# An S4 convolution block in float32 on one core: the prologue's step tables and sines in another order, the rows' first transform stage on 64 by 64 tiles, and the last block's inverse over all channels

## The chip, the cores and the metric

The kernel runs on one core of one Trainium2 chip. The metric is the device time of one execution in microseconds, as the median of several runs; the profile is one more execution with the hardware profiler on. PE is the matrix engine (PEld its weight loads), ACT, DVE and POOL are the scalar, vector and GpSimd engines, and SP issues most transfers. Each engine works through its own instruction list in order; engines wait for each other by semaphores.

## The reference, cut to what matters

A layer norm with a modulation from `silu(c) @ w_mod`, a long convolution per channel with a kernel `K` that is built from 192 complex modes, a residual, and then a second modulated layer norm with a bilinear GLU. L is 2048, D is 640, F is 1536.

```python
mod = (_silu(c) @ w_mod).reshape(c.shape[0], 6, 1, -1)
sa, ca, ga, sb, cb, gb = (mod[:, 0], ...)
h = _layernorm(x, axis=-1) * (1 + ca) + sa
# _A_ref(h): per channel d
dt = jnp.exp(log_dt)[:, None]
P = jnp.exp((dt * A)[:, :, None] * l[None, None, :])
K = jnp.einsum("dn,dnl,dn->dl", Cc, P, dt * Bc).real
y = irfft(rfft(h padded to 2L) * rfft(K padded to 2L))[:L] + h * Dskip
x = x + ga * y
h = _layernorm(x, axis=-1) * (1 + cb) + sb
x = x + gb * (((h @ w_gate) * (h @ w_up)) @ w_down)
```

## The kernel before

The 640 channels are five blocks (`db`) of 128. The 2L-point transform is done as two matrix stages, 32 by 64.

*Kernel generation.* For 40 groups `n` of 16 channels the values of `K` come from outer products of two short tables per channel: POOL multiplies out the phases (`mk_ph`, tile `Ph`) and the amplitudes (`mk_eq`, `mk_ep`, tiles `EQ` and `EP`, two buffers each, taken in turn), ACT takes sines and cosines of the phases (`trig`, PSUM tiles `tra` and `trb`), DVE multiplies amplitude and sine (tiles `QtA`, `PtA`, `QtB`, `PtB`), and PE contracts over the modes (`kg_ma`, `kg_mb`, tile `kg`). The short tables come from `u_seeds(db)`, once for each block: steps named by letters, in the order of the strings `SEG0` (block 0) and `SEG` (the others). `a` to `d` make the phase step, `r` and `R` the decay steps of the block's two halves, `e` and `E` their exponentials (`LP`, `RH`, `RL`), `x` to `f` the amplitude and the angle of a mode, `g` and `h` transpose them, and `v` turns them into the start values. `tab_ph` and `tab_eq` then double the steps into tables on POOL; `weighted` (lines 637 and 638) waits for `v` there.

*Rows.* `u_stats` loads a slab of x and takes its statistics on DVE, `u_hm` normalises it on ACT and stores it to `hm` in DRAM. `u_pre(db, q)` loads a quarter of a block from `hm` and runs the first stage of the row transform on PE: 32 by 32 tiles, for a real and an imaginary part, and the same again with one contraction row for the shift (`t_one`). The result goes to `FH` in DRAM. `u_g(db, qd)` reads a quarter of the frequencies back, runs the second stage (`stage2`, line 876) and keeps the spectra in place in the tile `gh` (three buffers).

*Product and way back.* `u_k(n)` is the first stage for `K`, into the tile `f16` (two buffers). `u_c(db, qd)` runs the second stage for `K`, multiplies with the row spectra on DVE (six operations, lines 911 to 922), runs the first inverse stage on PE (line 930), and writes to `WD` in DRAM. `u_d(db, c)` reads `WD` across, runs the last inverse stage (line 951), adds x and writes `x2d`. In the last block `u_c` is called twice for each quarter, for 64 channels each: eight units, each with its own second stage, product, inverse and write.

*GLU.* `u_head` loads the first four row slabs of `x2d` as `xb`, takes the remaining statistics when `u_d(4, 0)` has come, and starts the up projections (`psg`, lines 973 to 975). Then 48 rounds (line 1281) of up and down projections follow, each in three products of split operands.

*What sets the order.* The loop over `t` (line 1153) runs through the generation, three steps for each `n`. Everything else is cut at its `yield`s, and the table `SCHED` gives each piece a due time: `due(x)` (line 1084) issues all pieces whose time lies in bucket x, two buckets of ten for each step `t`. Times below zero lie in the prologue, one bucket for each step of `u_seeds(0)`; times from 2400 on lie behind the last generation step. `SLOT` gives the buffer letter of each allocation. So the table fixes, for each engine and for the transfer queues of SP and ACT, what is issued behind what.

## Time and profile before

| | us |
|---|---|
| median of the three runs | 1056.52 |
| the runs | 1050.58, 1058.03, 1056.52 |
| the profiled execution, its own time | 1050.8 |
| its span in the trace | 1049.0 |
| PE busy | 941.2 (90%) |
| DVE busy | 645.8 (62%) |
| ACT busy | 575.5 (55%) |
| POOL busy | 410.2 (39%) |

The shares of the whole span say little, because the kernel has four stages in a row: the prologue until the first sines (about 34 us), the generation with the transforms of the first four blocks beside it (to about 465 us), the rest of the last block and the head of the GLU (to 547 us), and the GLU rounds. In the last stage PE works without a gap, POOL works only up to the end of the generation.

The page's slices, 40 of 26 us each, show the four stages at a glance: for POOL the busy digits end where the generation ends, and the clock row shows where PE was granted less than full speed.

```profile
PE   4834899898789798998689999999999999999998
DVE  8678468797978997874555544535445263444242
ACT  4849989887888889852233244332443234433231
POOL 4976789699779989920026000000000000000000
PEclk9878699799889899998779999999999999999999
```

### The profile page before, as it was taken

The page shows a single profiled execution, that of the slowest core. Times are in us where ns is not written, and L with a number is a line of the kernel's source. Part 1 is how long each engine was busy: PE and PEld are TensorE (multiplying, and loading weights), DVE is VectorE, ACT ScalarE, POOL GpSimd, SP SyncE. Part 2 cuts the span into 40 slices and gives each one's busy share as a digit, 9 for nine tenths or more (in the row PEclk, how much of TensorE's full clock was granted, in tenths as well). Part 3 has the DMA queues.
Part 4 walks back from the last instruction along what each step waited for, and adds up shares of the span by engine and source line. Part 5 has one row for each costly group of instructions (what it writes and reads, how often), then busy time and mean ns, then how long its engine had stood idle before and what let it go on. Part 6 is the DMA issues. An engine that isn't in the chain of part 4 may idle for free.

```text
span 1049.0 us, 27184 instructions
## 1 busy us (share of the span) xinstructions
PE 941.2 (90%) x11750; PEld 771.4 (74%) x11750; DVE 645.8 (62%) x1216; ACT 575.5 (55%) x1027; POOL 410.2 (39%) x268
## 2 busy tenths in 40 slices
PE   4834899898789798998689999999999999999998
PEld 2623666676576577777548888888888888888887
DVE  8678468797978997874555544535445263444242
ACT  4849989887888889852233244332443234433231
POOL 4976789699779989920026000000000000000000
PEclk9878699799889899998779999999999999999999
DMA  7537657255435553577569000100002000010001
GB/s 252 215 88 249 209 186 223 68 156 157 130 115 163 163 169 109 168 224 216 148 197 367 24 1 1 62 39 1 1 1 101 1 1 1 1 51 1 1 1 51
DMA packets 118456, 113.00 MB, mean 108 GB/s; under 512 B 16192, under 2 KB 99904, under 8 KB 117696
## 3 DMA queue, kind: packets, MB, share of 16 engines
q1 hardware_dynamic: 108864, 108.25, 32.4%
q10 hardware_dynamic: 9472, 3.02, 1.1%
q8 instruction: 92, 1.51, 0.6%
q14 instruction: 28, 0.23, 0.1%
HBM read 74.48 MB, written 36.77 MB: 106 GB/s over the span
## 4 chain that ended last, share of the span: by engine, by line
PE 68%; ACT 15%; DVE 10%; issue 4%; DMA 3%; SPq 1%; DVEq 0%; ACTq 0%
PE acc L1256 16%; PE psg L973 11%; PE psg L975 10%; PE psg L974 10%; PE psfc L876 2%; PE psfb L876 2%; ACT trb L227 2%; ACT tra L227 2%; PE psfb L930 2%; ACT L227 2%; PE psfa L876 2%; PE psfc L930 1%; PE kg L809 1%; PE kg L794 1%; ACT LP L227 1%
## 5 line engine op out<-in xcount | busy, mean ns | idle before, releaser
L1233 DVE TENSOR_TENSOR pr<-psg,gsb 128x512 f32<-128x512 f32 x48 | 33.2, 691 | 203.5 <-issue 147.5
L697 POOL TENSOR_TENSOR EQ<-LQ,RH 128x1536 f32<-128x1536 f32 x40 | 124.3, 3106 | 20.6 <-DVE QtB L754 20.2
L227 ACT ACTIVATE ah<-pr 128x512 fp32r<-128x512 f32 x48 | 30.4, 632 | 150.9 <-DVE pr L1233 150.9
L973 PE MATMUL psg<-hh,wsgh 128*128 128x512 f32 x240 | 96.1, 401 | 1.0 <-ACT hh L227 1.0
L974 PE MATMUL psg<-hh,wsgl 128*128 128x512 f32 x240 | 94.1, 392 | 0.0
L975 PE MATMUL psg<-hl,wsgh 128*128 128x512 f32 x240 | 94.1, 392 | 0.0
L974 PE MATMUL psg<-hh,wsul 128*128 128x512 f32 x240 | 94.0, 392 | 0.0
L973 PE MATMUL psg<-hh,wsuh 128*128 128x512 f32 x240 | 93.9, 391 | 0.0
L975 PE MATMUL psg<-hl,wsuh 128*128 128x512 f32 x240 | 93.7, 391 | 0.0
L1256 PE MATMUL acc<-wsdl,ah 128*128 128x384 f32 (+1 forms) x384 | 88.2, 309 | 0.0
L1256 PE MATMUL acc<-wsdh,al 128*128 128x384 f32 (+1 forms) x384 | 88.1, 309 | 0.0
L1256 PE MATMUL acc<-wsdh,ah 128*128 128x384 f32 (+1 forms) x384 | 87.9, 308 | 0.0
L227 ACT ACTIVATE gsb<-psg 128x512 f32<-128x512 f32 x48 | 28.4, 592 | 99.3 <-PE psg L975 99.3
L697 POOL TENSOR_TENSOR EP<-LP,RH 128x768 f32<-128x768 f32 x40 | 66.1, 1653 | 0.0
L697 POOL TENSOR_TENSOR Pha<-LH,DH 128x1536 int32<-128x1536 int32 (+1 forms) x21 | 62.5, 2974 | 6.6 <-ACT trb L227 6.2
L1256 PEld LDWEIGHTS acc<-wsdh,ah 128*128 128x128 f32 x384 | 62.2, 188 | 3.8
L697 POOL TENSOR_TENSOR Phb<-LH,DH 128x1536 int32<-128x1536 int32 x20 | 62.3, 3115 | 1.8 <-ACT tra L227 1.8
L1256 PEld LDWEIGHTS acc<-wsdl,ah 128*128 128x128 f32 x384 | 58.9, 188 | 0.0
L1256 PEld LDWEIGHTS acc<-wsdh,al 128*128 128x128 f32 x384 | 58.8, 188 | 0.0
L968 DVE TENSOR_TENSOR al<-pr,ah 128x512 fp32r<-128x512 f32 x48 | 34.4, 717 | 33.5 <-ACT ah L227 33.5
L975 PEld LDWEIGHTS psg<-hl,wsgh 128*128 128x128 f32 x240 | 45.1, 188 | 10.9 <-DVE hl L1015 1.1
L809 PEld LDWEIGHTS kg<-QtB,PtB 64*32 64x32 f32 x2560 | 41.4, 113 | 15.6 <-issue 7.5
(516 smaller groups left out, 2523.8 us busy)
## 6 DMA issues: line engine op xcount, KB each, us to landing
TVa<-WD SPq DMA_DIRECT2D x28, 256.0 KB, 3.4
t_tw<-w_mod SPq DMA_DIRECT2D x3, 1600.0 KB, 7.9
t_ti<-w_mod SPq DMA_DIRECT2D x3, 1600.0 KB, 7.8
ghb<-FH SPq DMA_DIRECT2D x8, 512.0 KB, 4.7
WD<-Wb SPq DMA_DIRECT2D x8, 512.0 KB, 3.4
WD<-Wa SPq DMA_DIRECT2D x8, 512.0 KB, 4.0
wg<-B_w_gate SPq DMA_DIRECT2D x6, 640.0 KB, 9.5
wu<-B_w_up SPq DMA_DIRECT2D x6, 640.0 KB, 10.7
```

What stands on the lines that cost most here:

```text
L227: return S.activation(o, i, f, **kw)
L697: G.tensor_tensor(o.rearrange("p x (h l) -> p x h l", l=8), lo.unsqueeze(2).to_broadcast([P, rows, nh, 8]), hi.rearrange("p h x -> p x h") ...
L794: PE.matmul(kg[j * 32 : j * 32 + 32, dd, :], PtA[:, c, dl * 4 + j, :], QtA[:, c, dl * 4 + j, :], start=dd == 0 and c == 0, stop=False, til ...
L809: PE.matmul(kg[j * 32 : j * 32 + 32, dd, :], PtB[lo : lo + 64, c, r, :], QtB[lo : lo + 64, c, r, :], start=False, stop=dd == 7 and c == 1, ...
L876: PE.matmul(r[c][par * 64 : par * 64 + 64, i, :], t_tw[:, k0 + k, c, :], src[:, k, :], start=True, stop=True, tile_position=(0, par * 64))
L930: PE.matmul(r[par][:, i, :dn], t_ti[lo : lo + 64, qd * 4 + i, c, :], x[lo : lo + 64, i, :], start=n == 0, stop=n == len(pro) - 1, tile_pos ...
L968: V.tensor_tensor(lo, v, hi, op=OP.subtract)
L973: PE.matmul(ps, wh, xh, start=start, stop=False)
L974: PE.matmul(ps, wl, xh, start=False, stop=False)
L975: PE.matmul(ps, wh, xl, start=False, stop=stop)
L1233: V.tensor_tensor(pr, r[1], gsb, op=OP.mult)
L1256: PE.matmul(o[c], x[:, ts], w[:, cs], start=st, stop=ft == NF - 1 and n == 2 and (c == 0 or t % 2 == 1))
```

## The change

The change has four parts and a new table of due times.

1. *Prologue.* The step `E` (exponentials of block 0's second half) leaves the prologue and becomes a piece of its own (`LATE`, due at 150, in the generation's step 7). The amplitude is computed first in `s_f`; a new step `G` transposes it before the arctangent, and ACT instead of DVE copies it into `RL`. `tab_ph` computes the third phase step for only the half that it works on, so block 0 has one more short POOL operation. The identity matrix comes by a transfer of its own instead of an ACT copy, and the constants come in three transfers instead of one.
2. *Rows.* `u_pre` runs its first stage in 64 by 64 tiles with weights that hold two slabs each, eight products instead of sixteen for each quarter and block.
3. *Last block.* `u_c` is one unit for each quarter with two second stages and two products of 64 channels, written in place into the row spectra, and then one inverse, one evacuation and one write over all 128 channels. The row spectra of the last block lie in one `f16` buffer (`GL`) instead of four `gh` buffers.
4. *Order.* All due times and buffer letters are new. Of the table the diff below shows the due times of the seeds of blocks 2 and 3, one number for each step of `SEG`.

```diff
-SEG0 = ("l", "a", "b", "c", "ud", "r", "x", "e", "f", "g", "D", "h", "v", "R", "E")
+SEG0 = ("l", "a", "b", "c", "ud", "r", "x", "e", "f", "G", "g", "D", "h", "v", "R", "")
...
-    tab=(475, 761),
+    tab=(526, 788),
...
+    e0=(150,),
...
-        (375, 435, 587, 674, 684, 684, 716, 751, 825, 825, 844, 868, 874, 882),
-        (880, 973, 1167, 1241, 1254, 1260, 1312, 1324, 1350, 1355, 1358, 1358, 1360, 1369),
...
+        (375, 582, 589, 670, 671, 677, 723, 786, 824, 825, 826, 845, 861, 863),
+        (984, 1169, 1224, 1242, 1264, 1267, 1286, 1292, 1336, 1336, 1343, 1343, 1345, 1349),
...
+            V.scalar_tensor_tensor(amp, u, dt2[:, db : db + 1], pe[:, 1], op0=OP.mult, op1=OP.mult)
             V.scalar_tensor_tensor(pe[:, 0], pe[:, 0], 1e-37, u, op0=OP.max, op1=OP.add)
             V.reciprocal(pe[:, 0], pe[:, 0])
-            V.scalar_tensor_tensor(amp, u, dt2[:, db : db + 1], pe[:, 1], op0=OP.mult, op1=OP.mult)
...
-        def s_g():
+        def s_G():
...
             trans(amp, T["ps2"][:, 0])
+            if db == 0:
+                for h in range(2):
+                    act(g4(Rl[h])[:, 3], T["ps2"][:, 0, hs[h]])
+
+        def s_g():
+            if db:
+                s_G()
             act(y, y, AF.Arctan)
...
+        if db == 0:
+            LATE.append(lambda: s_e(1))
...
-        if a != 0:
-            G.tensor_tensor(dh[:, 3], dh[:, 1], dh[:, 2], op=OP.add)
+        G.tensor_tensor(sel(dh[:, 3]), sel(dh[:, 1]), sel(dh[:, 2]), op=OP.add)
...
-            for j in range(4):
-                a = slice(32 * j, 32 * j + 32 if i == 0 else 32 * j + 1)
+            for j in range(2):
+                a = slice(64 * j, 64 * j + 64 if i == 0 else 64 * j + 1)
                 for c in range(2):
-                    o = 32 * (j ^ (2 * c))
-                    PE.matmul(r[c][o : o + 32], (t_s1h, t_one)[i][a, c], h[a] if i == 0 else shr[a, d0].unsqueeze(1).to_broadcast([1, 4, P]),
-                              start=i == 0, stop=i == 1, tile_position=(32 * j, o))
+                    o = 64 * (j ^ c)
+                    PE.matmul(r[c][o : o + 64], (t_s1h, t_one)[i][a, c], h[a] if i == 0 else shr[a, d0].unsqueeze(1).to_broadcast([1, 4, P]),
+                              start=i == 0, stop=i == 1, tile_position=(64 * j, o))
...
-        Gt = ring(fp, [P, 8, P], "gh")
+        if db < NB - 1:
+            Gt = ring(fp, [P, 8, P], "gh")
+        else:
+            if db not in GL:
+                GL[db] = ring(f16, [P, 32, P], "f16")
+            Gt = GL[db][:, k0 : k0 + 8]
...
-    def u_c(db, qd, d0=0, d1=P):
+    def u_c(db, qd, parts=1):
+
+        k0, dn = 8 * qd, P // parts
+        for d0 in range(0, P, dn):
+            need(dn // 16, "F", db, d0)
...
+            kr, ki = stage2(FS[db][:, k0 : k0 + 8, d0 : d0 + dn], k0, r)
+            yield
...
+            x = T if parts == 1 else H
+            V.tensor_tensor(x[:, 0], T[:, 0], kr, op=OP.subtract)
+            V.tensor_tensor(x[:, 1], T[:, 1], ki, op=OP.add)
+            yield
+        if parts > 1:
+            x = GH[db, qd]
...
-        WQ[len(PF) - 1].dma_start(WD[db][:, k0 : k0 + 8, d0:d1], W.rearrange("p i r d -> p (i r) d"))
+        WQ[len(PF) - 1].dma_start(WD[db][:, k0 : k0 + 8], W.rearrange("p i r d -> p (i r) d"))
...
-            if db < NB - 1:
-                at(T0["c"][db][q], u_c, db, q)
-            else:
-                for h in range(2):
-                    at(T0["c"][db + h][q], u_c, db, q, h * P // 2, h * P // 2 + P // 2)
+            at(T0["c"][db][q], u_c, db, q, 1 if db < NB - 1 else 2)
...
-    SY.dma_start(ct, I["t_c"])
+    SY.dma_start(ct[:, 0:256], I["t_c"][:, 0:256])
+    SY.dma_start(ident, I["t_c"][:, 256:384])
+    SY.dma_start(ct[:, 256:], I["t_c"][:, 384:])
```

The new due times move work on all engines. Three places are shown, the second on two engines; the line numbers of the changed kernel are its own.

*First place, ACT at the end of the prologue.* `TVa` is a row of the modulation, `LP`, `RH` and `RL` are the exponentials of step `E`, `ab` and `trb` the first phases and their sine. Before:

```order
L227 ACTIVATE pta<-pta 128x192
L227 ACTIVATE TVb<-psfb 1x256
L227 ACTIVATE TVa<-psfa 1x384
L227 ACT_TABLE_LOAD
L227 ACTIVATE LP_148<-RL_158 128x96 x7
L227 ACTIVATE RH_155<-RH_155 128x1056
L227 ACTIVATE RL_158<-RL_158 128x288
L227 ACTIVATE ab<-Pha 128x512
L227 ACT_TABLE_LOAD
L227 ACTIVATE trb<-Pha 128x512
```

and after the change, where the two copies out of `tra` stand ahead of the arctangent:

```order
L228 ACTIVATE RL_157<-tra 128x96
L228 ACTIVATE RL_158<-tra 128x96
L228 ACT_TABLE_LOAD
L228 ACTIVATE pta<-pta 128x192
L228 ACTIVATE TVb<-psfb 1x256
L228 ACTIVATE TVa<-psfa 1x384
L228 ACTIVATE ab<-Pha 128x512
L228 ACT_TABLE_LOAD
L228 ACTIVATE trb<-Pha 128x512
```

The exponentials stand no longer ahead of the first sine. They come 28 instructions further down, behind the first four sines and cosines of `n`=2, with a table load on each side.

*Second place, DVE in the steps for `n`=2 and 3.* The statistics pairs (`BN_STATS`, `BN_AGGR`) each need a slab of x, in the buffer that the row names; the same buffer can be loaded again only after the pair before it. Before:

```order
L752 TENSOR_TENSOR QtA<-tra,EQ_143 128x32x32
L753 TENSOR_TENSOR QtA<-tra,EQ_143 128x16x32
L754 SCALAR_TENSOR_TENSOR QtA<-tra,EQ_143 128x16x32
L759 TENSOR_TENSOR PtAb<-trb,EP_145 128x1024
L469 BN_STATS st_812<-gha 128x6 x2
L470 BN_AGGR mv_95<-st_812 128x2
L469 BN_STATS st_825<-gha 128x6 x2
L470 BN_AGGR mv_95<-st_825 128x2
L469 BN_STATS st_829<-ghb 128x6 x2
L470 BN_AGGR mv_95<-st_829 128x2
L552 TENSOR_TENSOR pta<-psfb,ptb 128x384
```

and after the change, from the pair ahead of `PtB` on:

```order
L470 BN_STATS st_707<-gha 128x6 x2
L471 BN_AGGR mv_95<-st_707 128x2
L789 TENSOR_TENSOR PtB<-trb,EP_144 128x512
L762 TENSOR_TENSOR QtB<-trb,EQ_142 128x16x32
L763 TENSOR_TENSOR QtB<-trb,EQ_142 128x8x32
L764 SCALAR_TENSOR_TENSOR QtB<-trb,EQ_142 128x8x32
L762 TENSOR_TENSOR QtA<-tra,EQ_143 128x32x32
L763 TENSOR_TENSOR QtA<-tra,EQ_143 128x16x32
L764 SCALAR_TENSOR_TENSOR QtA<-tra,EQ_143 128x16x32
L470 BN_STATS st_762<-ghc 128x6 x2
L471 BN_AGGR mv_95<-st_762 128x2
L470 BN_STATS st_811<-gha 128x6 x2
```

Two pairs on the same buffer `gha` stood back to back; now seven products and a pair on `ghc` stand between them. From the `QtA` of `n`=2 to the `PtB` of `n`=3 there are seven pairs where there were six.

The slabs come on SP's queue. Behind block 1's seeds stood, before:

```order
L539 DMA pta<-A_A_im 128x192
L461 DMA ghb<-A_u 128x640
L461 DMA f16a<-A_u 128x640
L461 DMA gha<-A_u 128x640
L461 DMA ghc<-A_u 128x640 x2
L461 DMA gha<-A_u 128x640
L393 DMA dgd<-dcol 128x4x1
```

and after the change, where the weights of the fourth modulation vector (`t_ti<-w_mod`) have moved from ahead of those seeds to behind them:

```order
L540 DMA pta<-A_A_im 128x192
L353 DMA t_ti<-w_mod 128x5x640
L462 DMA ghc<-A_u 128x640
L462 DMA gha<-A_u 128x640
L462 DMA f16a<-A_u 128x640
L462 DMA Wb<-A_u 128x640
L394 DMA dgd<-dcol 128x4x1
```

Four slabs where there were six, and a read of 1600 KB in front of them.

*Third place, PE behind the end of the generation.* `f16b` holds the first stage of the last block's `K`, `64x64 x16` is a second stage over 64 channels, `t_ti` the inverse. Before, at the seam of two of the eight units:

```order
L930 MATMUL psfc<-TVb,t_ti 128x64
L930 MATMUL psfa<-TVb,t_ti 128x64
L876 MATMUL psfc<-f16b,t_tw 64x64 x16
L930 MATMUL psfa<-TVb,t_ti 128x64
L930 MATMUL psfb<-TVb,t_ti 128x64
```

and after the change, up to the first of the four inverses:

```order
L886 MATMUL psfa<-f16b,t_tw 64x64 x16
L841 MATMUL psfb<-ct,Ktb 64x128 x8
L964 MATMUL psfc<-TVa,ct 32x512 x4
L886 MATMUL psfb<-f16b,t_tw 64x64 x16
L886 MATMUL psfa<-f16b,t_tw 64x64 x16
L943 MATMUL psfc<-f16a,t_ti 128x128
L943 MATMUL psfb<-f16a,t_ti 128x128
```

A second stage stood between every two inverses, eight times; now six of the eight second stages are issued before the first inverse, and four inverses of twice the width follow with two second stages between them. On ACT's transfer queue eight writes to `WD` of 64 channels become four of 128.

More of the change, by code (lines that the diff above doesn't have):

```diff
@@ L75 @@
-    q=(
[4 rows of a table removed]
+    ml=(-885, -911, -989),
+    mr=(((-871, 89), (-871, 110)), ((-874, 26), (-884, 85)), ((-886, -866), (-888, -871))),
+    st=(
+        (-881, 51),
+        (-1006, -914),
+        (51, 229),
+        (-884, 159),
+        (-983, 0),
+        (104, 215),
+        (-936, -871),
+        (-978, -871),
+        (17, 200),
+        (3, 193),
+        (-911, -870),
+        (-883, 63),
+        (-871, 131),
+        (-990, -906),
+        (-883, 169),
+        (-984, -870),
+    ),
+    hm=(
+        (-1010, 359),
+        (261, 368),
+        (157, 359),
+        (45, 328),
+        (-988, 315),
+        (32, 242),
+        (303, 330),
+        (-877, 240),
+        (214, 259),
+        (147, 306),
+        (259, 375),
+        (324, 407),
+        (425, 536),
+        (528, 544),
+        (445, 539),
+        (356, 434),
+    ),
@@ L145 @@
-    low=((153, 435, 642, 889, 1136, 1387, 1591, 1856, 2077), (198, 403, 681, 934, 1166, 1410, 1612, 1874, 2120)),
-    w=(2548, 2440, 2834, 2848),
-    h=(2793, 2860, 2874, 2876, 2876, 2876, 2878, 2879),
-    g=(
[5 rows of a table removed]
[5 rows of a table added]
+    ),
+    c=(
[5 rows of a table added]
+    ),
+    d=(
[5 rows of a table added]
+    ),
+    k=(
+        (167, 177),
+        (309, 391),
+        (675, 710),
+        (452, 511),
+        (433, 460),
+        (480, 518),
+        (603, 619),
+        (619, 664),
+        (674, 699),
+        (829, 839),
+        (902, 909),
+        (1092, 1097),
+        (956, 974),
+        (969, 1054),
+        (1067, 1070),
+        (1080, 1080),
+        (1260, 1292),
+        (1259, 1267),
+        (1453, 1476),
+        (1414, 1426),
+        (1473, 1485),
+        (1417, 1434),
+        (1505, 1574),
+        (1489, 1495),
+        (1606, 1624),
+        (1687, 1714),
+        (1877, 1897),
+        (1882, 1908),
+        (2012, 2039),
+        (2018, 2077),
+        (1960, 1963),
+        (1984, 2016),
+        (2097, 2137),
+        (2350, 2377),
+        (2212, 2252),
+        (2289, 2315),
+        (2481, 2546),
+        (2430, 2519),
+        (2474, 2543),
+        (2515, 2552),
+    ),
@@ L185, in _tables @@
     f = np.stack([np.cos(al), -np.sin(al)], 0)
-    s1h = np.tile(f.transpose(1, 0, 2).reshape(1, 32, 64), (4, 1, 1))
-    one = np.tile(f.sum(1).reshape(1, 64), (128, 1))
+    s1h = np.zeros((2, 2, 32, 2, 2, 32))
+    for q in range(2):
+        s1h[:, q, :, :, q] = f.transpose(1, 0, 2)
+    one = np.tile(f.sum(1).reshape(1, 2, 1, 32), (128, 1, 2, 1))
     ib = np.tile(f.transpose(0, 2, 1).reshape(1, 64, 32) / 2048, (2, 1, 1))
@@ L473, in u_hm @@
     def u_hm(q):
-        if q >= 6:
-            XT[q] = x_load(q)
+        x = x_load(q) if q >= 6 else None
         yield
-        x = XT[q]
+        if q < 6:
+            x = XT[q]
         need(1, "rs", q < 6)
@@ L630, in s_v @@
             ps = T["ps2"]
-            for h in range(2):
-                V.tensor_copy(g4(Rl[h])[:, 3], ps[:, 0, hs[h]])
+            if db:
+                for h in range(2):
+                    V.tensor_copy(g4(Rl[h])[:, 3], ps[:, 0, hs[h]])
             V.tensor_scalar(psi, ps[:, 1], 4294967296.0 / math.pi, None, op0=OP.mult)
```

165 lines of the change are left out of this document (39 added, 126 removed), and 45 rows, old and new, of tables (c, d, g, pre).

## The prediction

> **What bounds the kernel now.** I read the busy time by stage first, then the list of waits for POOL, then the timelines at the three places where everybody stands still. The columns are start and end, length, busy time (and instructions) of PE, PEld, DVE, ACT and POOL, the granted clock, DMA share and GB/s.
>
> ```profile
> 0.00:34.00 34.00, 16.60 (x55) 10.69 (x56) 25.37 (x102) 19.48 (x39) 20.06 (x28) 0.95 0.83 285
> 34.00:66.00 32.00, 24.01 (x487) 19.59 (x485) 28.88 (x60) 23.32 (x42) 31.61 (x21) 0.95 0.42 138
> 66.00:76.00 10.00, 0.15 (x1) 0.18 (x2) 4.57 (x13) 0.58 (x3) 5.34 (x3) 0.53 0.17 34
> 300.00:452.00 152.00, 135.25 (x3418) 101.69 (x3412) 133.72 (x216) 129.73 (x228) 145.60 (x84) 0.96 0.53 159
> 480.00:518.00 38.00, 31.62 (x508) 27.88 (x508) 21.98 (x62) 7.62 (x20) 0.00 (x0) 0.86 0.60 170
> 518.00:547.00 29.00, 21.37 (x90) 10.24 (x82) 14.35 (x32) 10.42 (x21) 4.88 (x10) 0.66 0.58 161
> 547.00:1049.00 502.00, 497.66 (x2624) 440.24 (x2622) 227.79 (x392) 178.35 (x314) 20.58 (x12) 1.00 0.11 40
> ...
> POOL EQ L697 <- DVE QtB L754: 20.2, 5, 11.2
> POOL DL L638 <- issue: 17.9, 3, 10.8
> ```
>
> From 547 us on PE is full for 502 us at full clock; the change does not touch these rounds, so they stay and all gains lie ahead of 547. Between 34 and 452 us POOL is nearly full wherever nothing stops it (31.61 of 32, 145.60 of 152), with PE, DVE and ACT at 85 to 90%. So the generation runs at POOL's pace, and it loses time where POOL stands: the last two rows (total, times, longest) say 20.2 us for an `EQ` buffer that DVE had not used up, and 17.9 us for the start values of a block. Behind 465 us there is no POOL work; between 480 and 518 us no engine is full, a sign of a chain of latencies.
>
> **Part 1, the prologue.** How the first sine and the first DVE product come about:
>
> ```profile
> 9.82 0.89 DVE L469 BATCH_NORM_STATS2 st<-Wa 128x6 f32<-128x320 f32 x2 [0.83 <-DMA Wa<-A_u]
> 27.14 3.09 POOL L697 TENSOR_TENSOR EQ<-LQ,RH 128x1536 f32<-128x1536 f32 x1
> 26.67 0.48 ACT L227 ACTIVATE TVa<-psfa 1x384 f32<-1x384 f32 x1 [2.85 <-PE psfa L359]
> 27.17 1.28 ACT L227 ACT_TABLE_LOAD   x1
> 28.46 1.42 ACT L227 ACTIVATE LP<-RL 128x96 f32<-128x96 f32 x7
> 30.99 0.62 ACT L227 ACTIVATE ab<-Pha 128x512 f32<-128x512 int32 x1
> 31.61 1.28 ACT L227 ACT_TABLE_LOAD   x1
> 32.91 0.60 ACT L227 ACTIVATE trb<-Pha 128x512 f32<-128x512 int32 x1
> ```
>
> ACT loses its exponentials between 27.17 and 30.99, 3.8 us, so `trb` could come 3.8 us earlier. But its product also needs `EQ`, which POOL finishes at 30.2, and POOL, not ACT, is full from then on. So I count what POOL gains. The statistics pair at 9.82 stood ahead of the phase steps (0.83 wait, 0.89 and the aggregate, near 2 us); it goes behind them, and POOL's chain moves 2 us forward. The added short POOL operation costs back about 0.4. I take 1.5 us, between 0 (if the matmul rows of the modulation, which now stand ahead of the first `kg`, hold PE) and 3.8. The exponentials return in step 7 with one table load more than before: 1.28 us by the rows above. ACT is busy 23.32 of 32 us there and waits for POOL's tiles, so I cost the 6.5 us at nothing; if that cover is gone they cost up to 6.5. The transfers (three for one) are two issues of about 0.5 us on SP; two slabs fewer stand ahead of the modulation's first read, which gives that back.
>
> The Trainium skill (ScalarE: Activation LUTs, section What ACT_TABLE_LOAD costs) gives a switch 1.28 us for the load plus 1.38 us for a drain; the rows agree with the load and show no drain, since `LP` starts 0.01 us behind it. By the page the extra load would cost 2.66 us, still under ACT's idle time.
>
> **Part 4, order: the stop at 66 us.** This is the longest wait of POOL:
>
> ```profile
> 59.16 0.68 DVE L779 TENSOR_TENSOR PtB<-trb,EP 128x512 f32<-128x512 f32 x1
> 63.78 0.68 DVE L754 SCALAR_TENSOR_TENSOR QtA<-tra,EQ 128x512 f32<-128x512 f32 x1
> 66.41 0.33 SPq L461 DMA_DIRECT2D gha<-A_u  x1
> 71.88 0.89 DVE L469 BATCH_NORM_STATS2 st<-gha 128x6 f32<-128x320 f32 x2 [5.25 <-DMA gha<-A_u]
> 75.65 0.36 ACT L227 ACTIVATE ptb<-ptb 128x192 f32<-128x192 f32 x1 [9.42 <-issue]
> 82.52 3.10 POOL L697 TENSOR_TENSOR EQ<-LQ,RH 128x1536 f32<-128x1536 f32 x1 [11.18 <-DVE QtB L754]
> ```
>
> DVE finished a statistics pair on `gha`, and its next instruction was a pair on the same buffer, whose load could only then be issued, at 66.41. It landed 5.25 us later; behind it on DVE stood two pairs more and block 1's step `b`, for which ACT waited 9.42 us, and `PtB` and `QtB`, for which POOL waited 11.18. After the change the reload of `gha` is issued behind the pair ahead of `PtB`, and from the start of `PtB` (59.16) to the end of that `QtA` (64.4) there are 5.2 us of DVE work, with another pair of 1.1 us: 6.3 us against a landing of 5.5. So the 5.25 us go; one pair more in the same stretch gives 1.1 back: 4.1 us. What can eat it is the transfer queue: now a read of the modulation weights stands just ahead of these slabs on SP.
>
> ```profile
> t_ti<-w_mod SPq DMA_DIRECT2D x3, 1600.0 KB, 7.8
> ```
>
> It takes 7.8 us to land, and slabs behind it on the same queue hardly land sooner. How early it is issued in its new place the trace of before cannot show, so I take 3 us for this place, between -3 (the slabs late by the whole read) and 9.4 (the stop gone with all that hangs on it). Next in line there is ACT's list of normalisations.
>
> **Part 4, order: the start values.** POOL's second kind of stop:
>
> ```profile
> 294.97 0.39 POOL L638 TENSOR_TENSOR DL<-ptb 128x96 int32<-128x96 int32 x1 [10.78 <-issue]
> ```
>
> POOL's own order does not change here. The last steps of block 2's and block 3's seeds (`g` to `v`, and for block 3 from `e` on) are due 13 to 23 units earlier against it, 20 units being one step of the generation, about 3.6 us (430 us for 120 steps). POOL's stop at 295 shrinks from 10.8 to about 7, the one before block 2 by as much; the third stays. ACT does the same table loads and exponentials, so part of this comes back as a wait for ACT. I take 5 us, between 0 and 7.
>
> All other pieces of the generation stand in another order too. Which new waits that makes no row shows. I bound it by what POOL lost on `EQ` buffers apart from the stop at 66 us, 9 us each way, and take nothing.
>
> **Part 2, rows.** One quarter's first stage, first and last of 32 records (each product is two):
>
> ```profile
> 337.70 1.01 PE L855 MATMUL psfa<-hfb,ct 32*32 32x512 f32 x2 [0.49 <-DVE TVb L921]
> 339.66 0.59 PE L855 MATMUL psfb<-shr,ct 1*32 1x512 f32 x1
> ```
>
> From 337.70 to 340.25 is 2.55 us for 32 records of 0.59 us, so eight run side by side, in four waves of 0.43 us. In 64 by 64 tiles there are 16 records on four different tiles; if those run side by side it is four waves again, with half the weight loads. I cost the part at nothing, with 20 units times 0.3 us at most to gain, hidden under POOL. The other end stands with the rivals.
>
> **Part 3, the last block.** The way from the first product to the first `xb`:
>
> ```profile
> 477.14 0.41 DVE L911 TENSOR_TENSOR TVb<-psfc,ghc 128x256 f32<-128x256 f32 x1
> 482.52 0.42 DVE L911 TENSOR_TENSOR TVb<-psfb,ghb 128x256 f32<-128x256 f32 x1 [2.31 <-PE psfa L930]
> 493.33 0.42 DVE L911 TENSOR_TENSOR TVb<-psfa,gha 128x256 f32<-128x256 f32 x1 [3.63 <-PE psfc L930]
> 513.63 0.41 DVE L922 TENSOR_TENSOR TVa<-TVa,psfb 128x256 f32<-128x256 f32 x1
> 517.82 0.38 ACT L227 ACTIVATE Wa<-psfa 128x256 f32<-128x256 f32 x1
> 518.23 2.58 DMA WD<-Wa
> 521.01 2.99 DMA TVa<-WD
> 524.13 2.71 PE psfc L951 x8
> ...
> 480.00:518.00 38.00, 19.80 (x256) 18.69 (x256) 0.86 0.60 170
> 340.96 0.48 PE L930 MATMUL psfa<-TVb,t_ti 64*128 64x128 f32 x2 [0.71 <-ACT hfa L227]
> 343.11 0.38 PE L930 MATMUL psfb<-TVb,t_ti 64*128 64x128 f32 x2
> ```
>
> Eight units of six DVE operations run from 477.14 to 514.0. One unit is 2.45 us (477.14 to 479.5), so 19.6 us are work, and the rest is mostly DVE waiting for a second stage that stands behind an inverse. The last three rows price the inverse: 19.8 us of PE for the eight units of 64 columns, 2.5 each (the window row holds line 930 alone), and the same 2.5 us for a unit of 128 columns in the generation (340.96 to 343.49). Four units take 10 us instead of 19.8.
>
> By the new order the first unit is done before the last wait for block 3's `u_d`; seven units (17 us), one `u_d` addition (0.7), the last inverse (2.5) and its evacuation (1.1) follow it: 21 us. Before, from the same wait to the last evacuation, it was 477.1 to 518.2, 41 us. The difference is 20. Against it stand waits that remain: the second stages of the last three units share banks with inverses and evacuations, each worth one of the waits above, 2 us on average; with two of them 16 us are left. A write of twice the size may land up to 1.5 us later than 2.58. I take 16, between 6 (every unit still waits as before) and 20. Behind it, from `xb` to 547, nothing gets shorter. The row spectra now wait for `f16`'s old content, block 3's last second stage on PE, some three steps (11 us) ahead of the generation's end; that covers their landing of about 5 us. If it doesn't, they are next to be late.
>
> **The sum.** 1.5 + 3 + 5 + 0 + 0 + 16 = 25.5 us less than the profiled execution's 1050.8, so 1025. That execution lies below two of the three runs (1058.0 and 1056.5; median 1056.5), whose rounds are the same, so a median some 4 us above the profiled sum is as likely as not: I predict 1029.
>
> **The rivals.**
>
> - *Only the tail moves.* The generation's new order makes as many stops as it takes away, since PE, DVE and ACT have little room at 85 to 90%. For it: 145.60 of 152 us are POOL's already. Against: two of the stops had one visible cause. Time: 1050.8 - 16 + 4 = 1039.
> - *The tail's gain is eaten.* The row spectra or block 3's `u_d` come late, and the eight products start 10 us later. For it: SP works in order, and the reads of the spectra stand ahead of those of `u_d`. Time: 1050.8 - 6 + 4 = 1049, no change.
> - *Slower: the 64 by 64 products do not run side by side.* If only two of the four tiles run at a time, a unit takes eight waves, 1.7 us more, 34 us over 20 units; one after another it is 12 waves more, 5.2 us, 103 us over all. PE has about 10% free in the generation, which I do not count. It decides the sign from about 1.2 us a unit on. With two at a time 1025 + 34 + 4 = 1063, one at a time about 1130. Against it: 32-row tiles ran eight at a time here, and 64-row ones two at a time (line 930: 32 records in 2.5 us). No run here shows a 64 by 64 tile.
>
> The Trainium skill (TensorEngine Tiling (Array Packing), section Available Configurations) counts four independent tiles in 64 by 64 mode and 16 in 32 by 32; by that this rival falls. No trace so far shows it.
>
> **How the numbers follow.** The forecast 0.60, only the tail 0.20, tail eaten 0.12, slower 0.08. A difference under 1% is about what a measurement of this kernel cannot tell from none, so "faster" is below 1046, "same" 1046 to 1067. The forecast and the tail alone give faster, 0.80; the eaten tail and the slower rival's mild form give same, 0.14; slower 0.06. The range: the low end has the full 20, 9.4 and 7 us, 1050.8 - 38 = 1012; the high end takes in the tail alone and the start of the eaten tail, 1048.
>
> **What would show it.** Part 1: the first `QtA` near 30 us instead of 34.34, and POOL's first whole `EQ` near 25.6. The stop: no stretch between 60 and 80 us in which ACT, PE and DVE all stand. Start values: a longest wait of `DL` near 7. Rows: a unit of line 865 at 2.5 us or less; above 3.7 the slower rival holds. Tail: the last evacuation to `WD` 37 us behind the generation's end (465.5) instead of 53. The prediction is wrong if the generation ends later than 465 us, or if DVE's product units still stand apart by 4 us and more.

## The result, and the profile after

| | before | after |
|---|---|---|
| median, us | 1054.58 | 1024.03 |
| runs, us | 1050.58, 1058.03, 1056.52, 1052.63 | 1017.94, 1029.56, 1019.87, 1028.18 |
| profiled execution, its span | 1050.8, 1049.0 | 1017.94, 1016.2 |

The ratio is 0.971, with a 95% interval from 0.963 to 0.979: faster by 2.9%. The predicted 1029 stands 5 us above the median, inside the range.

The stages of after, as the windows give them, with the columns as before:

```profile
66.00:76.00 10.00, 2.75 (x98) 2.25 (x102) 8.05 (x29) 5.86 (x10) 4.53 (x3) 0.83 0.36 60
464.00:484.00 20.00, 16.26 (x322) 14.25 (x322) 18.33 (x45) 5.79 (x10) 0.00 (x0) 1.00 0.84 265
484.00:492.60 8.60, 2.56 (x37) 1.53 (x34) 4.62 (x19) 3.10 (x4) 0.00 (x0) 0.79 0.62 217
492.60:521.60 29.00, 26.84 (x114) 14.49 (x115) 17.60 (x35) 11.29 (x22) 10.26 (x13) 0.83 0.73 220
521.60:1016.20 494.60, 490.23 (x2592) 434.32 (x2590) 225.21 (x388) 175.99 (x310) 16.75 (x10) 1.00 0.10 35
```

The GLU rounds, from the first down projection to the end, take 494.6 us, as they did before (554.4 to 1049.0). So the whole 32.8 us lies ahead of them. In the stretch from 66 to 76 us DVE is busy for 8.05 of 10 us, where it was 4.57 and PE stood. In the last block's way back (464 to 484) DVE is nearly full, where no engine was.

The loss of the generation is read from the waits of POOL between 45 and 460 us (total, times, longest). First the rows of before that were not shown yet, which go with the 20.2 us for `EQ` and the 17.9 us for `DL`:

```profile
POOL Pha L697 <- ACT trb L227: 6.2, 4, 2.7
POOL LQ L691 <- DVE RL L632: 2.7, 1, 2.7
POOL Phb L697 <- ACT tra L227: 1.8, 1, 1.8
```

And all of after:

```profile
POOL EQ L707 <- DVE QtB L764: 15.8, 6, 5.5
POOL DL L647 <- issue: 9.7, 2, 8.1
POOL LQ L701 <- DVE RL L641: 4.0, 1, 4.0
POOL Phb L707 <- ACT tra L228: 2.3, 2, 1.9
POOL Pha L707 <- ACT trb L228: 2.0, 3, 1.0
```

With two waits of before for loads, 0.9 us together, the sums are 49.7 and 33.8 us. POOL's last `EQ` came 17.5 us earlier (430.10 instead of 447.63): 15.9 us are these waits, 1.2 the prologue. Behind that `EQ`, up to the first down projection, it took 91.3 us instead of 106.7, which are the other 15.4 us. POOL's last `EQ` is the better boundary between generation and tail: the last product `kg`, which the prediction used, came 17.7 us behind it before and 24.1 us after, because a part of the last block's second stage now runs ahead of it. Line 886 (876 before) alone, from the last `kg` to the first down projection, before and then after:

```profile
465.50:554.40 88.90, 17.45 (x384) 15.75 (x384) 0.83 0.68 202
```

```profile
454.50:521.60 67.10, 11.61 (x288) 10.63 (x288) 0.90 0.77 238
```

Of 384 products 288 are left behind the boundary, 5.8 us of PE less.

### The profile page after: what moved, and what is told of

Same layout as the page of the kernel before. It is cut to its first block, busy times and chain, and to the rows that moved or that the text cites. A ratio compares the mean times of both kernels' runs of the same rounds, so it can differ in the third digit from the quotient of the medians.

```text
span 1016.2 us, 26287 instructions
## 1 busy us (share of the span) xinstructions
PE 914.6 (90%) x11302; PEld 748.2 (74%) x11302; DVE 646.9 (64%) x1214; ACT 574.9 (57%) x1020; POOL 411.6 (41%) x269
## 4 chain that ended last, share of the span: by engine, by line
PE 64%; ACT 14%; DVE 11%; DMA 4%; issue 4%; POOL 2%; SPq 0%; DVEq 0%; ACTq 0%; POOLq 0%
PE acc L1266 17%; PE psg L986 11%; PE psg L988 11%; PE psg L987 11%; ACT trb L228 2%; ACT tra L228 2%; ACT L228 2%; PE kg L804 1%; PE kg L819 1%; PE psfb L886 1%; PE psfc L886 1%; DMA TVb<-WD 1%; PE psfb L943 1%; PE psfa L943 1%; DVE QtA L762 1%
## 5 line engine op out<-in xcount | busy, mean ns | idle before, releaser
L819 PE MATMUL kg<-QtB,PtB 64*32 64x64 f32 x2560 | 48.1, 227 | 7.3 <-DVE QtB L763 7.2
```

The lines of the kernel that those rows point to most:

```text
L819: PE.matmul(kg[j * 32 : j * 32 + 32, dd, :], PtB[lo : lo + 64, c, r, :], QtB[lo : lo + 64, c, r, :], start=False, stop=dd == 7 and c == 1, ...
```

## Experiments

The table has the profiled execution's landmarks in us (the start of POOL's last `EQ`, of the last `kg` product, of the first down projection) and the timed ratio to the kernel before on the same chip. Kernels that ran on different chips are compared by the ratio. `after` and `c_after_again` are the same program: from one profiled execution to the other its last `EQ` differs by 4.8 us and its first down projection by 7.7. So a smaller difference of landmarks between two kernels shows nothing by itself.

| kernel | last EQ | last kg | first down | median | ratio, 95% |
|---|---|---|---|---|---|
| before | 447.6 | 465.3 | 554.3 | 1054.58 | |
| after | 430.1 | 454.2 | 521.4 | 1024.03 | 0.971 (0.963 to 0.979) |
| e4_no_stop | 441.2 | 459.7 | 547.9 | 1043.19 | 0.987 (0.979 to 0.995) |
| e2_new_tail_alone | 452.9 | 483.1 | 550.8 | 1047.83 | 0.992 (0.987 to 0.996) |
| e3_old_tail | 435.2 | 463.0 | 551.4 | 1051.49 | 0.995 (0.992 to 0.999) |
| e1_rows32 | 439.2 | 465.1 | 535.6 | 1031.31 | 0.973 (0.967 to 0.979) |
| c_after_again | 434.9 | 460.5 | 529.1 | 1026.86 | 0.973 (0.969 to 0.977) |
| e9_fold_in_psum | 435.9 | 461.8 | 529.2 | 1023.11 | 0.970 (0.966 to 0.974) |
| e6_exp_early | 436.7 | 462.7 | 529.8 | 1024.84 | 0.970 (0.965 to 0.976) |
| e7_half_inverse | 430.7 | 456.3 | 542.0 | 1038.58 | 0.984 (0.979 to 0.988) |
| e5b_seeds_late | 445.9 | 470.4 | 538.1 | 1034.14 | 0.980 (0.976 to 0.984) |
| e8b_seeds_early | 450.4 | 475.8 | 542.5 | 1037.58 | 0.982 (0.977 to 0.988) |
| e5_seeds_late | 450.6 | 478.6 | 558.8 | 1055.16 | 1.000 (0.997 to 1.003) |
| e8_seeds_early | 450.1 | 479.9 | 561.0 | 1057.35 | 1.002 (0.999 to 1.005) |

**e4_no_stop: two due times in the kernel before.** The statistics pair of slab 9 moves ahead, and that of slab 6, whose load was issued too late, moves behind two others, so that the pairs on `gha` no longer stand back to back; nothing else changes.

```diff
-        (-881, 220),
+        (-881, 228),
...
-        (33, 217),
+        (33, 188),
```

> The kernel before with two numbers changed: the statistics pair of slab 9 ahead of the QtA of 62 us, that of slab 6 behind those of slabs 7 and 8, so that the reload of the one buffer no longer stands between two neighbours on DVE. Theory (the stop at 66 us has this one cause and POOL sets the pace): POOL's wait of 11.2 us at 82.5 falls to 5 to 7, POOL's EQ there starts 4 to 6 us earlier, and the last kg product comes 3 to 6 us earlier than 465.5. Rival (what POOL gains there it loses later to the same waits): the EQ of 82.5 comes earlier, but the last kg product stays within 1.5 us of 465.5.

Measured: 0.987. The timeline of POOL shows that `EQ`:

```profile
78.17 3.10 POOL L592 TENSOR_TENSOR EQ<-LQ,RH 128x1536 f32<-128x1536 f32 x1 [6.21 <-DVE QtB L649]
```

It starts 4.35 us earlier than before (82.52), and its wait is 6.21 instead of 11.18 us. The last `kg` comes 5.6 us earlier and the first down projection 6.4. So the stop was the late load, as the prediction read it. The ratio, with an interval from 0.979 to 0.995 (some 5 to 22 us), says that a gain reaches the end; its size is not settled, and one of the four runs (1055.63) lies among those of before.

**e5_seeds_late and e5b_seeds_late: the last steps of the seeds of blocks 2 and 3 at their old due times, in after.** Both have the due times below, and e9's fold (further down) as well.

```diff
-        (375, 582, 589, 670, 671, 677, 723, 786, 824, 825, 826, 845, 861, 863),
-        (984, 1169, 1224, 1242, 1264, 1267, 1286, 1292, 1336, 1336, 1343, 1343, 1345, 1349),
+        (375, 582, 589, 670, 671, 677, 723, 786, 824, 825, 844, 868, 874, 882),
+        (984, 1169, 1224, 1242, 1264, 1267, 1286, 1292, 1336, 1355, 1358, 1358, 1360, 1369),
```

> The changed kernel, fold in PSUM, with the last steps of block 2's and block 3's start values (from f, and from eE, on) due as late as before the change (18 to 23 units, one step of the generation). Theory (the prediction's start values, 5 us): POOL's wait for DL at block 2 comes back with 4 to 5 us, that at block 3 grows from 8.1 to 10 to 11, POOL's last EQ comes 5 to 7 us later, and the time is 3 to 7 us longer than with the fold in PSUM alone. Rival A (what POOL loses there it makes up in the waits behind): POOL's last EQ within 2 us. Rival B (POOL is late, but the last block's work behind its last EQ is what sets the end): POOL's last EQ 5 us later, the first down projection within 2 us.

> The late start values once more (last steps of block 2's and 3's start values due as before the change, fold in PSUM), now with each tile in the PSUM bank that it has in the changed kernel: the first version handed out 74 of 271 bank letters anew, and its tail, which holds none of the moved steps, grew from 67 to 80 us. Theory (POOL's waits for DL are the price of the late steps; the rest of the 30 us were the letters): POOL's last EQ 5 to 12 us later than 435.9, the last part from the last kg product to the first down projection 66 to 69 us, the time 4 to 12 us above the fold in PSUM alone. Rival (the late steps cost the 30 us by themselves): the last part stays at 80 us, the time at 1050 and more.

In e5 the buffer letters were dealt out afresh along the new order, and 74 of the 271 letters of the PSUM banks `psf` came out other than in e9. It ran as long as the kernel before (1.000), and even its tail, which the seeds do not touch, took 80.2 us from the last `kg` instead of e9's 67.4. In e5b all letters but three are e9's, and the tail is 67.7. The two kernels differ in nothing but 71 letters, and 2% of the time hang on them: a letter decides which older user of a bank an operation waits for.

So e5b is the test of the seeds. Against e9 the ratio rises from 0.970 to 0.980, POOL's last `EQ` comes 10.0 us later and the first down projection 8.9. POOL's waits for the start values, first in e9, then in e5b:

```profile
POOL DL L649 <- issue: 9.1, 2, 7.5
```

```profile
POOL DL L542 <- issue: 22.5, 3, 12.1
```

By these landmarks the seeds' due times are worth 9 to 10 us, by the medians 11 (1034.14 and 1023.11), about twice the 5 us of the prediction; the two intervals of the ratio do not overlap.

**e8_seeds_early and e8b_seeds_early: block 3's seeds earlier still.** From step `x` on 40 units (two generation steps) ahead of after, the four steps before it 15 to 25; again on e9.

```diff
-        (984, 1169, 1224, 1242, 1264, 1267, 1286, 1292, 1336, 1336, 1343, 1343, 1345, 1349),
+        (984, 1169, 1224, 1242, 1246, 1252, 1264, 1267, 1296, 1296, 1303, 1303, 1305, 1309),
```

> The changed kernel, fold in PSUM, with the steps of block 3's start values from r on due 40 units (two steps of the generation, 7.2 us) earlier, against POOL's wait of 8.1 us at 278.6. Theory (the wait is the lateness of these steps and nothing else): the wait falls to about 1, POOL's last EQ comes 5 to 7 us earlier, the time is 3 to 7 us shorter than with the fold in PSUM alone. Rival (the steps cannot start earlier, because what they overwrite is still read, or they push other work of ACT and DVE back): the wait stays above 5, or POOL waits as long for an EQ or a Ph instead.

> The early start values of block 3 once more (steps from r on two steps of the generation earlier, fold in PSUM), with the bank letters of the changed kernel but for 8 of 271. In the first version the wait of 8.1 us for DL was gone, and POOL waited 8.4 us more for EQ and Phb in the same place. Theory (with the letters kept these waits go, and the gain of the DL wait stays): POOL's last EQ 3 to 7 us earlier than 435.9, the time 2 to 7 us below the fold in PSUM alone. Rival (ACT and DVE have no room for the steps there, whatever the letters): POOL's last EQ later than 435.9, and no gain in the time.

e8 had 75 letters other than e9 and went the way of e5. e8b has eight, and its waits of POOL are:

```profile
POOL EQ L602 <- DVE QtB L659: 32.7, 8, 7.3
POOL Phb L602 <- ACT tra L121: 11.6, 3, 9.3
...
POOL DL L542 <- issue: 1.6, 1, 1.6
```

The stop on `DL` is gone (9.1 to 1.6), but POOL now waits 32.7 us for `EQ` buffers (17.6 in e9) and 11.6 for a phase buffer. Its last `EQ` is 14.5 us later. With these earlier due times the wait of 8 us that is left in after brought nothing: POOL waited for DVE and ACT instead, as the rival said. Other due times were not tried, and eight letters differ here too.

**e2_new_tail_alone and e3_old_tail: the last block by itself.** e2 puts part 3 and the due times of the last block's pieces into the kernel before; e3 takes them out of after. At the seam some due times had to follow, and 39 (e2) and 32 (e3) letters of `psf`, 6 and 9 of `TV`, are other than in the kernel each was made from. Of e2, the unit and one row of its due times:

```diff
-    def u_c(db, qd, d0=0, d1=P):
+    def u_c(db, qd, parts=1):
...
-        ((2123, 2262, 2265), (2277, 2316, 2350), (2324, 2375, 2427), (2109, 2123, 2145)),
+        ((2123, 2262, 2265), (2277, 2316, 2350), (2324, 2375, 2400), (2109, 2123, 2145)),
```

> The kernel before, with only the last block's way back as in the change (four units with two products each, one inverse and one write a quarter, row spectra in one buffer, and the steps behind about 2400 in the new order); prologue, rows and the generation's order are the old ones. Theory (the tail is a term of its own, 21.8 us by the two traces: from the last kg product to the first down projection 88.9 us before, 67.1 after): the last kg product stays at 465.5 within 2, from there to the first down projection 67 to 70 us, span 1027 to 1031 in place of 1049.0. Prediction as it stood: 16 us, span 1033. Rival (the short tail needs the generation's new order): 76 us and more, span above 1036.

> The changed kernel with the last block's old way back (eight units of half the channels, each with its own inverse and write, row spectra in four buffers, the last steps in the old order); prologue, rows and the generation's order are the new ones. Theory (generation and tail add up): the last kg product at 454.5 within 2, from there to the first down projection 86 to 90 us, span 1035 to 1040. Rival (both depend on each other): the last kg product comes more than 3 us later than 454.5, or the tail is shorter than 80.

From the last `kg` to the first down projection the tails are 67.7 us in e2 (67.2 in after) and 88.4 in e3 (89.0 before), as the expectations had them. But the last `kg` itself is late in both: 483.1 us in e2 where 465.5 was expected, and 463.0 in e3 where 454.5 was (c has it at 460.5). Counted from POOL's last `EQ`, the better boundary, the new tail is 97.9 us in e2 and the old one 116.2 in e3, against 106.7 before and 91.3 to 94.2 in the two profiles of the changed kernel. So the new tail saves 8.8 us behind the old generation and 22 to 25 behind the new one, and the totals do not add up: 0.8% and 0.5%, and 2.9% for both. The rivals, by which the parts depend on each other, have e2's span (1045.4, above their 1036) and e3's last `kg` for them. In e2 the last `kg` comes 30.2 us behind POOL's last `EQ` (17.7 before, 24.1 after), and the waits of PE from 440 to 500 us have

```profile
PE psfb L846 <- issue: 7.1, 2, 3.6
```

two stops of some 3.5 us ahead of products of the last inverse stage, at 457 and 470 us, ahead of the last `kg` in PE's list. Which part of this the seam makes and which the new letters, these two runs do not tell: e5 shows that letters alone can cost as much.

**e1_rows32: after with the rows' first stage on 32 by 32 tiles.**

```diff
-            for j in range(2):
-                a = slice(64 * j, 64 * j + 64 if i == 0 else 64 * j + 1)
+            for j in range(4):
+                a = slice(32 * j, 32 * j + 32 if i == 0 else 32 * j + 1)
...
-                    o = 64 * (j ^ c)
+                    o = 32 * (j ^ (2 * c))
```

> The changed kernel with the rows' first stage back on 32 by 32 tiles (32 products a unit in place of 16); all else stays. Theory (the prediction's part 2, worth nothing either way): a unit of products takes about 2.5 us in both shapes, the last kg product stays at 454.5 us within 1.5, and the time stays within 5 us of the changed kernel's (span 1016.2 in its profile). Rival A (half the products and weight loads free PE, 0.3 us a unit, 20 units): the last kg product at 457 to 461. Rival B (64 by 64 tiles run only two at a time and cost 1.7 us a unit, and other things paid for it): with 32 by 32 tiles the last kg product comes before 451.

The ratio is 0.973, that of after within the interval. The line's own windows, after (one unit, then all 20) and e1 (all 20):

```profile
316.00:319.00 3.00, 2.11 (x16) 0.44 (x16) 1.00 0.00 0
100.00:470.00 370.00, 46.45 (x320) 9.89 (x320) 0.95 0.54 167
```

```profile
100.00:470.00 370.00, 44.43 (x640) 11.55 (x640) 0.94 0.54 166
```

16 products of 64 by 64 take PE 2.11 us, and 20 units 46.5 us; 32 products of 32 by 32 take 44.4 us for all units. Part 2 shows no gain and no loss, within the some 8 us that the two intervals leave. The expectation missed the last `kg` (465.1 instead of 454.5), but most of that is not the rows' doing: 5.3 of the 9.1 us at the last `EQ` stood at the fifth `EQ` (67.64 instead of 62.36 us), ahead of the first unit of rows. The next pair is about that difference.

**c_after_again and e9_fold_in_psum.** c is after, unchanged. e9 has another form of `u_fold`, the eleven small operations that fold the modulation into the columns: intermediate values go to PSUM, so that no operation reads two operands from SBUF, with one operation more.

```diff
+        qg, gp = pc[:, 16 : 16 + NB], pc[:, 24 : 24 + NB]
...
-        V.tensor_tensor(g1, g1, sg, op=OP.mult)
+        V.tensor_tensor(qg, qg, sg, op=OP.mult)
...
-        V.tensor_tensor(dcol[:, 1:], dcol[:, 1:], gg[:, 1:], op=OP.mult)
+        V.tensor_tensor(gp, p3[:, 2], g1, op=OP.mult)
+        V.tensor_tensor(dcol[:, 1:], dcol[:, 1:], gp[:, 1:], op=OP.mult)
```

> The changed kernel once more, unchanged, for the spread of its own landmarks. In three other runs the ten small DVE operations of the fold of the modulation took 5 to 6 us longer than in the two traces compared so far (one 128x5 operation 3.00 us in place of 0.23), ending with a long operation of POOL. Theory (they wait for POOL's operation whenever they fall into one, and a transfer that lands 1 us later decides it): the first EQ operations within 0.3 us of the changed kernel's; if the fold takes about 2.4 us, the last kg product is near 454, if it takes 6 to 8, it is 5 to 10 us later. Rival (the runs differ by the granted clock): the fold is short and the landmarks drift apart evenly over the generation.

> The changed kernel with the fold's intermediate values in PSUM, so that none of its small DVE operations but the reciprocal has two inputs in SBUF or goes from SBUF to SBUF (one operation more, 0.16 us). Theory (an operation of DVE with two inputs in SBUF waits until POOL's running operation ends): each of these operations takes 0.15 to 0.35 us wherever POOL is, the fold under 3 us, the last kg product at 450 to 457, and the median of the time 4 to 8 us below that of the unchanged kernel on this chip. Rival (the long operations have another cause, such as a semaphore or the transfers): operations of 1 us and more are still there.

The fold on DVE and POOL in c, from the timeline:

```profile
51.44 0.16 DVE L389 TENSOR_TENSOR mcol<-psfb,mcol 128x5 f32<-128x5 f32 x1
52.58 3.09 POOL L707 TENSOR_TENSOR EQ<-LQ,RH 128x1536 f32<-128x1536 f32 x1
52.63 3.06 DVE L393 TENSOR_TENSOR dcol<-dcol,mcol 128x4 f32<-128x4 f32 x1
```

An operation on 128 by 4 elements takes 3.06 us, and ends when POOL's long one beside it ends (55.69 and 55.67). The one that reads a PSUM operand takes 0.16. In e9 the same last operation is

```profile
51.41 0.15 DVE L395 TENSOR_TENSOR dcol<-dcol,psfb 128x4 f32<-128x4 f32 x1
```

and the fifth `EQ` starts at 62.45 us, 65.83 in c. On the same chip e9's runs (1021.98 to 1025.71) lie below those of c (1025.61 to 1030.13) but for a tenth, and its median is 3.8 us lower: the fastest version tried. The two profiles, though, end alike (spans 1023.9 and 1023.8), because e9's gave the 3.4 us back in small waits by the last `EQ`. The expectation had 4 to 8 us, and a last `kg` at 450 to 457 (461.8). That the fold's stall costs 3.4 us where it stands is shown; how much of it reaches the end is not settled beyond the medians.

**e6_exp_early: e9 with the second exponentials back in the prologue.**

```diff
-SEG0 = ("l", "a", "b", "c", "ud", "r", "x", "e", "f", "G", "g", "D", "h", "v", "R", "")
+SEG0 = ("l", "a", "b", "c", "ud", "r", "x", "e", "f", "G", "g", "D", "h", "v", "R", "E")
...
-    at(T0["e0"], once(lambda: LATE.pop()()))
```

> The changed kernel, fold in PSUM, with the second exponentials (step E) back in the prologue, as before the change. Theory (the prediction's part 1: POOL, not ACT, sets the prologue; the exponentials are hidden either way): ACT's first trb 3 to 4 us later than 27.9, DVE's first QtA 3 to 4 us later than 30.4, but POOL's EQ operations of 25.9 to 62.4 stay within 0.5 us and the last kg product within 2 us of the fold in PSUM alone. Rival (the late exponentials are what the prologue gains): POOL's EQ operations from the third on come 2 us or more later, and the last kg product 3 to 4 us later.

The first block's products in e6 and, for comparison, in after:

```profile
25.97 3.10 POOL L709 TENSOR_TENSOR EQ<-LQ,RH 128x1536 f32<-128x1536 f32 x1
...
33.77 1.22 DVE L764 TENSOR_TENSOR QtA<-trb,EQ 128x1024 f32<-128x1024 f32 x1 [3.12 <-ACT trb L228]
```

```profile
25.90 3.09 POOL L707 TENSOR_TENSOR EQ<-LQ,RH 128x1536 f32<-128x1536 f32 x1
...
30.44 1.18 DVE L762 TENSOR_TENSOR QtA<-trb,EQ 128x1024 f32<-128x1024 f32 x1
```

DVE starts 3.3 us later, but POOL's second `EQ` stands at 32.09 (32.16 in e9), its third at 40.22 (39.89), and the first down projection is 0.6 us later than e9's. Medians are 1024.84 and 1023.11, with runs that overlap. Moving `E` takes 3 us off ACT's prologue and, within the spread of these runs, nothing off the kernel.

**e7_half_inverse: e9 with the inverse of each unit in two halves of 64 channels,** where the last block had them before; all else of part 3 stays.

```diff
+        for d0 in range(0, P, dn):
-                    PE.matmul(r[par][:, i], t_ti[lo : lo + 64, qd * 4 + i, c, :], x[lo : lo + 64, c, i, :], start=c == 0, stop=c == 1, tile_position=(lo, 0))
+                        PE.matmul(r[par][:, i, d0 : d0 + dn], t_ti[lo : lo + 64, qd * 4 + i, c, :], x[lo : lo + 64, c, i, d0 : d0 + dn], start=c == 0, stop=c == 1, tile_position=(lo, 0))
```

> The changed kernel, fold in PSUM, with the last block's inverse in two halves of 64 channels (64 products a quarter in place of 32), behind both products as now; one write a quarter as now. Theory (an inverse costs 2.5 us of PE whatever its width, so four fewer save 10 us of PE, and the last of them stands on the path): from the last kg product to the first down projection 3 to 6 us longer than in the fold in PSUM alone: 2.5 us for the last inverse, and something for the three others, which stand behind DVE's products. Rival A (PE has room there): only the last inverse counts, 2 to 3 us. Rival B (all 10 us count): 8 us and more.

The tail is 18.3 us longer than e9's (85.7 and 67.4) and the ratio 0.984 against 0.970. The inverse's busy time on PE from 456 to 540 us, e7 and then e9:

```profile
sum 84.00, PE 27.68 PEld 26.82; mean PE 27.68 PEld 26.82
```

```profile
sum 84.00, PE 9.77 PEld 8.92; mean PE 9.77 PEld 8.92
```

The tail grows by as much as these products (17.9 us), as rival B had it; the theory's 3 to 6 us were far too few. Twice the products at e9's time for one would be 19.5; the other 8 us go with a lower clock (last section). From before to after the same inverse fell from 21.9 to 8.6 us, 13.3 of the 15 to 22 us by which the tail got shorter. So fewer inverse products are the greater part of what part 3 brings behind the new generation; fewer waits between the units are left as the smaller, by difference and not by a run.

## Why the prediction was right or wrong

The time lies inside the range, and the places named in the prediction moved the way it said; the start values were set too small. But two things make the sum look better founded than it is. First, the sizes below come from the profile of after, the fastest of its four runs. The profile of c, the same program, ends 25.2 us ahead of that of before and not 32.8: 12.7 instead of 17.5 us at POOL's last `EQ`, 12.5 instead of 15.4 behind it. By the medians the gain is 30.6 us (30.1 on c's chip), 5 more than the sum's 25.5. That c's profile meets the sum is partly luck, since it holds 3.5 us of the fold's stall, for which the prediction has no term. Second, the sum adds generation and tail as if each had its own price. In e2 and e3 it has not: with other letters at the seam they brought 0.8% and 0.5%.

- *Prologue, predicted 1.5 (0 to 3.8).* POOL's first whole `EQ` starts at 25.90, predicted near 25.6 (27.14 before, so 1.24 us), and the first `QtA` at 30.44, predicted near 30. In step 7 the exponentials with both table loads take ACT 5.2 us (46.77 to 50.72, and 1.28 at 55.13), not 6.5, and by e6 it makes no clear difference to the kernel where they stand.
- *The stop at 66 us, predicted 3 (-3 to 9.4).* In after the `EQ` behind it starts at 75.59 instead of 82.52, 6.9 us earlier, of which 5.7 are not the prologue's. In c the same `EQ` is only 1.9 us earlier than before.

```profile
75.59 3.11 POOL L707 TENSOR_TENSOR EQ<-LQ,RH 128x1536 f32<-128x1536 f32 x1 [5.47 <-DVE QtB L764]
```

```profile
80.66 3.10 POOL L707 TENSOR_TENSOR EQ<-LQ,RH 128x1536 f32<-128x1536 f32 x1 [7.06 <-DVE QtB L764]
```

In c the fold had already cost 3.5 us at the fifth `EQ`, and the wait is 1.6 us longer. So one execution gave more than the 3 us and one less. The prediction counted 4.1 us, which e4 bears out with 4.35, and took off 1.1 for the read of the modulation weights ahead of the slabs. That read stands there in after and not in e4; no run prices it.
- *Start values, predicted 5 (0 to 7).* Too small. The stop at 295 is 8.09 us at 278.61, not 7, and that before block 2 (4.88 us at 204.30) is gone, not 1.3: together 7.6 us, as much as the prediction's two times 3.8. e5b prices the due times at 9 to 11 us. The step that failed is the deduction, "part of this comes back as a wait for ACT", some 2 us: the waits for ACT (`Pha` and `Phb`) fell too, from 8.0 to 4.3 us.

```profile
278.61 0.39 POOL L647 TENSOR_TENSOR DL<-ptb 128x96 int32<-128x96 int32 x1 [8.09 <-issue]
```

  "The third stays" held under another name. Before block 4 the tables `DL` and `LQ` have changed places in POOL's list, and the stop moved from the one to the other, before and then after:

```profile
376.36 0.39 POOL L638 TENSOR_TENSOR DL<-ptb 128x96 int32<-128x96 int32 x1 [2.29 <-issue]
```

```profile
358.39 0.36 POOL L701 COPY LQ<-RL 128x96 f32<-128x96 f32 x1 [3.98 <-DVE RL L641]
```

  Before block 1 it is the reverse: 2.75 us for `LQ` at 110.93, then 1.63 for `DL` at 103.09. So a fall of `DL` alone (17.9 to 9.7) says too much; with `LQ` the stops before the four blocks fell by 7.0 us, from 20.7 to 13.7.

- *The other order, 0 within 9.* The 17.5 us at the last `EQ` less 1.2, 5.7 and 7.0 leave 3.6 us.
- *Rows, 0.* Right by e1, and the slower rival falls: a unit takes 2.1 to 2.3 us where the prediction's price for two at a time was 1.7 us more. That price was too low: four waves in 2.55 us are 0.64 us each by its own row, not 0.43, so four waves more would be some 2.6 us. The Trainium skill (TensorEngine Tiling (Array Packing), section Available Configurations) counts four tiles of 64 by 64; the 2.11 us for 16 products, each some 0.6 us long, agree.
- *The last block, predicted 16 (6 to 20).* 15.4 us behind POOL's last `EQ` (12.5 in c), 21.8 behind the last `kg` (20.4 in c). The way there in after, from DVE's timeline (the first, second and last of the seven product units behind the last `kg`), and from the chain:

```profile
464.79 0.41 DVE L927 TENSOR_TENSOR TVb<-psfc,f16a 128x256 f32<-128x256 f32 x1
467.53 0.42 DVE L927 TENSOR_TENSOR TVb<-psfa,f16a 128x256 f32<-128x256 f32 x1 [0.20 <-DVE f16a L933]
...
480.82 0.42 DVE L927 TENSOR_TENSOR TVb<-psfc,f16a 128x256 f32<-128x256 f32 x1
```

```profile
486.07 0.60 ACT Wa L228
...
486.69 2.70 DMA WD<-Wa
...
489.51 3.00 DMA TVb<-WD
```

The units stand 2.5 to 3.0 us apart, so the two remaining waits of 2 us that were deducted did not come. The last evacuation ends 32.2 us behind the last `kg`, predicted 37, 53 before; second-stage products worth 5.8 us of PE had moved ahead of that `kg`. The write of twice the size lands after 2.70 us (2.58 before), so the 1.5 us feared for it were 0.1.
- *The generation's end.* Predicted no later than 465: 454.2. The sum of 25.5 was 32.8 in the profiled executions; stop (2.7) and start values (2.0) are 4.7 of the 7.3 us that the sum lacked there.
- *The rivals.* "Only the tail moves" fell with POOL's waits (15.9 us less). "The tail's gain is eaten" did not happen in after; e2 shows that something like it happens when the tail's new order stands behind the old generation's.

## What to carry to other kernels

Split a prediction at the engine that sets the pace (here POOL's last table) and not at a product whose place the change itself moves. When work is reordered under hand-dealt buffers, hold the letters fixed in a comparison and test them by themselves: here 71 letters were worth 2% of the time, where the whole change brought 2.9%. Profile the changed kernel twice before reading its landmarks: here they moved by up to 7.7 us. Where a product's time does not fall with its columns, as for the inverse here, halving the number of products at least halves their time (27.68 us in e7, 9.77 in e9).

## What the runs showed of the hardware

*Small DVE operations wait for POOL as busy time.* In c four of the fold's operations, with every operand in SBUF, took 0.56, 0.81, 0.93 and 3.06 us, each ending within 0.03 us of an operation of POOL. Others with every operand in SBUF, three of them begun where one POOL operation followed another, took 0.15 to 0.19, as those with an operand in PSUM did; in e9 all took 0.15 to 0.19. The lost time shows up as long operations and not as waits. In after the fold began at 47.05, beside short POOL operations, and took 0.15 to 0.32 each, so the same program differs by 3.5 us at the fifth `EQ` from one execution to another. The Trainium skill (SBUF — State Buffer, section Who interferes with whom) says that a VectorE instruction with two SBUF inputs contends with a GpSimd instruction that reads SBUF, and that the shared port pair is an exclusive lock; c's 3.06 us beside POOL's 3.09 agree. The operations of 0.56 and 0.81 us have one tensor input.

*Float32 products of 64 columns cost what those of 128 cost, and ran at a lower clock.* Line 946 of e7 by form: the shortest, median and longest duration in ns, then the span of starts and the shape.

```profile
L946 PE MATMUL psfb<-f16a,t_ti x128: 272/417/473, 474.1 to 505.6; 64*128 64x64 f32 x128
```

The shortest is 272 ns, as for 128 columns in the same line of the generation. The median of 417 goes with the granted clock, in e7 and then in after:

```profile
480.00:512.00 32.00, 26.97 (x262) 24.50 (x259) 9.50 (x31) 6.46 (x10) 0.00 (x0) 0.50 0.31 114
```

```profile
480.00:512.00 32.00, 23.33 (x174) 12.20 (x170) 20.14 (x55) 11.09 (x23) 4.91 (x10) 0.79 0.63 201
```

PE is busy for 26.97 of 32 us in e7 and gets half the clock; after is busy for less and gets 0.79. What sets the clock there was not tried.
